# Moving one attention step, one output copy, two matmul slices and one transpose in a fused retention and hard-swish MLP kernel

## The chip, the core and the metric

The kernel runs on one NeuronCore of a Trainium2 chip. The metric is the device time of one execution in microseconds, and the number compared is the median of several runs. TensorE (PE) multiplies matrices and writes to PSUM banks; VectorE (DVE) and ScalarE (ACT) work elementwise and copy PSUM to SBUF; GpSimd (POOL) issues the loads, which change float32 to float16 on the way; SyncE (SP) issues the stores and the transposing DMAs. Each engine runs its own list of instructions in order, and semaphores make one wait for another.

## The reference

Two stages in a row. The first is attention with a decay in place of a softmax (retention), for 8 batches, 8 heads, 576 positions and head size 64. Its output is the input of a two-layer MLP over 4608 tokens, with model width 512 and hidden width 2048:

```python
scores = scale * np.matmul(q, k.transpose(0, 1, 3, 2))
gamma = 1.0 - 2.0 ** (-5.0 - np.arange(H, dtype=np.float32))
rel = pos[:, None] - pos[None, :]
Dmat = np.where(rel >= 0, gamma[:, None, None] ** rel[None, :, :], 0.0)
x = np.matmul(scores * Dmat, v)          # reordered to (tokens, heads * head_dim)
h = x @ w_in
g = h * np.clip(h + 3.0, 0.0, 6.0) / 6.0
out = g @ w_out
```

## The kernel before

**Pieces and blocks.** Each batch's first 512 positions are cut into four pieces of 128; the last 64 positions of two batches make up one "rest" piece. Pieces 0 to 3 are batch 0, pieces 4 to 7 batch 1, pieces 8 to 11 batch 2, piece 12 the first rest piece. A block is 512 tokens: block 0 is pieces 0 to 3, block 1 is pieces 4 to 7. The attention of a piece writes its columns of `xt16`, the transposed input of the MLP, and a block can run when its four pieces stand there.

**Attention of one piece.** `transpose_k` and `transpose_q` (a DMA transpose on SP's queue, the second behind a scaling of Q and V on VectorE) or `k_by_pe` and `q_by_pe` (on TensorE, with a copy on ScalarE) bring K and Q into the tile `qk`. `scores` multiplies them into the PSUM tile `sc`; VectorE masks it into `at`; `intra` multiplies `at` with the scaled V (`vs`) into the PSUM tile `o`, which has one bank; the state of the earlier pieces (`tbd`) times Q is added to `o`; ScalarE copies `o` to `xt16` (L340). `update_mm` and `update_state` make the next state: matmuls into `u`, VectorE for `ta` and `ts`, then two ScalarE copies into a `tbd` tile (L387, L388).

**MLP of one block.** GEMM1 makes 16 hidden slices of 128 (`fc` 0 to 15): four matmuls into a bank of the PSUM tag `ph` (four banks), then a ScalarE activation and a VectorE product into `gt16`. GEMM2 makes four row tiles (`mc`), each of 16 matmuls, cut into four units of four (`part`); the last unit of a row tile is followed by a ScalarE copy to `osb` and a store on SP's queue. `put` runs a list of units, after each one at most one deferred piece of work (`run_later(1)`), and then the steps that stand under that unit's number.

**The order around the change.** While GEMM2 of block 0 runs, `first_step(c)` for c = 3 to 8 carries pieces 4 to 7 through the attention. Such a step finishes piece c - 1 (`intra`, `update_mm`, `update_state`, then the state matmuls at L550 and the copy), makes the scores of piece c, and prepares Q and K of piece c + 1. State copies and masks are put on the list `later` and come into the order of the engines when `run_later` is called. `first_step(7)` stands behind unit 15, the last of GEMM2 of block 0. Behind it come fc 0 and fc 1 of block 1 over the first 384 columns (`g1_columns` with `done`; these are pieces 4 to 6), then `first_step(8)`, which finishes piece 7, and then the rest of the first four slices, where `last` is piece 7's 128 columns. Fc 4 to 15 follow in `gemm1(1, ...)`, each with 512 columns; fc 4 takes the bank of fc 0. The transposes for pieces 8 and later go through SP's queue in program order, between the stores.

## Time and profile before

| what | value |
|---|---|
| three runs | 310.9, 312.09, 312.16 us; median 312.09 us |
| profiled execution, its own time | 311.0 us |
| its span, first to last instruction | 309.2 us |
| mean granted TensorE clock | 0.992 |
| VectorE, ScalarE, GpSimd busy | 60%, 56%, 35% of the span |

A profile is one execution, recorded by the hardware. Its time is 1.8 us more than its span, and lies 1.1 us under the median of the three runs. A busy row of TensorE includes the time until the last result is out, so that rows that follow each other overlap by about 0.2 us. The granted clock is the share of its full speed that TensorE was allowed in a stretch.

### The profile page before, as it was taken

The page shows a single profiled execution, that of the slowest core. Times are in us where ns is not written, and L with a number is a line of the kernel's source. Part 1 is how long each engine was busy: PE and PEld are TensorE (multiplying, and loading weights), DVE is VectorE, ACT ScalarE, POOL GpSimd, SP SyncE. Part 2 cuts the span into 40 slices and gives each one's busy share as a digit, 9 for nine tenths or more (in the row PEclk, how much of TensorE's full clock was granted, in tenths as well). Part 3 has the DMA queues.
Part 4 walks back from the last instruction along what each step waited for, and adds up shares of the span by engine and source line. Part 5 has one row for each costly group of instructions (what it writes and reads, how often), then busy time and mean ns, then how long its engine had stood idle before and what let it go on. Part 6 is the DMA issues. An engine that isn't in the chain of part 4 may idle for free.

```text
span 309.2 us, 5776 instructions
## 1 busy us (share of the span) xinstructions
PE 299.3 (97%) x2239; PEld 150.4 (49%) x2239; DVE 185.6 (60%) x309; ACT 174.4 (56%) x301; POOL 107.9 (35%) x134
## 2 busy tenths in 40 slices
PE   6999997999999999999999999999999999999994
PEld 2644454544544554445544644455445544444443
DVE  4768336497747872885578747857688347207700
ACT  5568357484457564854574737644774567227611
POOL 8963577536522392045333750158000000000000
PEclk9999999799999999999999999999999999999998
DMA  9999999999999999639999997199930120010022
GB/s 69 148 194 204 190 165 204 174 163 83 154 182 119 98 153 156 128 22 158 145 151 104 130 173 146 18 146 146 139 85 34 70 68 2 34 68 36 1 68 68
DMA packets 153163, 35.51 MB, mean 115 GB/s; under 512 B 143792, under 2 KB 148656, under 8 KB 153136
## 3 DMA queue, kind: packets, MB, share of 16 engines
q0 software_dynamic: 117264, 18.36, 82.1%
q1 hardware_dynamic: 35472, 16.26, 26.5%
q10 hardware_dynamic: 400, 0.52, 0.5%
q8 instruction: 17, 0.28, 0.4%
q14 instruction: 10, 0.08, 0.1%
HBM read 36.70 MB, written 9.44 MB: 149 GB/s over the span
## 4 chain that ended last, share of the span: by engine, by line
PE 93%; ACT 3%; DMA 1%; DVE 1%; issue 0%; POOL 0%; POOLq 0%; DVEq 0%; ACTq 0%
PE ph L400 39%; PE pout L458 39%; PE o L334 3%; PE sc L301 2%; PE o L323 2%; DMA qv<-in_q_dram 1%; PE u L358 1%; PE pout L471 1%; PE ph L423 1%; PE trq L224 1%; PE sc L571 1%; ACT qk L230 1%; ACT xt L340 1%; PE trk L215 0%; DVE at L244 0%
## 5 line engine op out<-in xcount | busy, mean ns | idle before, releaser
L408 DVE SCALAR_TENSOR_TENSOR gt<-u,ph 128x512 f16<-128x512 f32 x144 | 98.1, 687 | 64.5 <-ACT u L407 63.8
L458 PE MATMUL pout<-wout,gt 128*128 128x512 f16 x560 | 125.8, 379 | 0.0
L400 PE MATMUL ph<-xt,win 128*128 128x512 f16 x560 | 122.4, 379 | 0.2 <-DVE gt L408 0.2
L407 ACT ACTIVATE u<-ph,cb 128x512 f32<-128x512 f32 x144 | 98.3, 687 | 26.0 <-PE ph L400 24.3
L400 PEld LDWEIGHTS <-win 128*128 128x128 f16 x560 | 54.6, 98 | 66.2 <-DMA win<-in_moe_w_in_dram 0.4
L458 PEld LDWEIGHTS <-gt 128*128 128x128 f16 x560 | 52.7, 98 | 61.1
L91 POOL DMA_DIRECT2D kn<-in_k_dram x40 | 34.6, 867 | 96.0 <-PE u L358 76.9
L462 ACT COPY osb<-pout 128x512 f32<-128x512 f32 x35 | 20.5, 586 | 48.9 <-PE pout L458 48.6
L305 DVE TENSOR_TENSOR at<-sc,mask_wide 128x1024 f16<-128x1024 f32 x19 | 23.2, 1222 | 27.2 <-PE sc L301 27.1
L91 POOL DMA_DIRECT2D qv<-in_q_dram x40 | 34.5, 866 | 4.4 <-DMA wout<-in_moe_w_out_dram 3.1
L91 POOL DMA_DIRECT2D qv<-in_v_dram x40 | 34.6, 872 | 2.8 <-DMA wout<-in_moe_w_out_dram 1.7
L387 ACT COPY tbd<-ts 64x256 f16<-64x256 f16 x28 | 11.3, 405 | 33.7 <-DVE ts L371 16.9
L340 ACT CAST xt<-o 128x512 f16<-128x512 f32 x35 | 19.4, 588 | 7.5 <-PE o L334 4.1
L291 DVE TENSOR_TENSOR vs<-qv,gqv 128x1024 f16<-128x1024 f16 x28 | 17.9, 685 | 3.2 <-DMA qv<-in_v_dram 3.2
L579 DVE TENSOR_TENSOR at<-sc,mask_wide 128x512 f16<-128x512 f32 x24 | 15.3, 681 | 0.0
L334 PE MATMUL o<-at,vs 128*64 128x128 f16 x280 | 12.4, 225 | 0.2
L374 DVE TENSOR_TENSOR ta<-u,ts 128x256 f32<-128x256 f32 x21 | 8.7, 415 | 5.0 <-PE u L358 5.0
L388 ACT COPY tbd<-ts 64x256 f16<-64x256 f16 x28 | 11.2, 401 | 0.4
L334 PEld LDWEIGHTS <-vs 128*64 128x64 f16 x280 | 8.9, 111 | 3.8 <-DVE vs L202 1.3
L375 DVE TENSOR_TENSOR ts<-ta,gc 128x256 f16<-128x256 f32 x21 | 8.9, 425 | 1.7
L301 PE MATMUL sc<-qk 64*128 64x128 f16 x184 | 9.3, 222 | 0.6 <-ACT qk L230 0.5
L323 PEld LDWEIGHTS <-tbd 128*128 128x128 f16 x112 | 7.0, 98 | 4.0
(69 smaller groups left out, 119.3 us busy)
## 6 DMA issues: line engine op xcount, KB each, us to landing
out_dram<-osb SPq DMA_DIRECT2D x32, 256.0 KB, 4.2
kn<-in_k_dram POOLq DMA_DIRECT2D x32, 128.0 KB, 4.5
qv<-in_q_dram POOLq DMA_DIRECT2D x32, 128.0 KB, 4.8
qv<-in_v_dram POOLq DMA_DIRECT2D x32, 128.0 KB, 5.4
wout<-in_moe_w_out_dram POOLq DMA_DIRECT2D x4, 512.0 KB, 15.1
win<-in_moe_w_in_dram POOLq DMA_DIRECT2D x3, 512.0 KB, 10.0
win<-in_moe_w_in_dram POOLq DMA_DIRECT2D x2, 256.0 KB, 5.9
kn<-in_k_dram POOLq DMA_DIRECT2D x8, 64.0 KB, 4.5
```

Of the source, the lines that this page charges most:

```text
L91: nc.gpsimd.dma_start(dst[p0:p0 + n], src[b, :, s0:s0 + n, :].rearrange("h s d -> s h d"))
L291: nc.vector.tensor_tensor(out=vs, in0=loaded[c]["qv"], in1=gqv, op=ALU.mult)
L301: nc.tensor.matmul(sc[:, h2, p, :], qk[r, 1, p, :], qk[r, 0, p, :], start=True, stop=True)
L305: later.append(lambda: nc.vector.tensor_tensor(out=at.rearrange("t a b s -> t (a b) s"), in0=sc.rearrange("t a b s -> t (a b) s"), in1=mas ...
L334: nc.tensor.matmul(o[r, p, :], vs[:, 2 * p + h2, :], at[:, h2, p, :], start=(st[c]["first"] and p == 0), stop=(p == NPAIR - 1 and not more ...
L340: nc.scalar.copy(xt16[:, :, g0:g0 + P], o)
L400: nc.tensor.matmul(ph, win16[:, dmc, P * fc:P * fc + P], xt16[:, dmc, t0:t0 + MBLK], start=(dmc == 0), stop=(dmc == NCC - 1))
L407: nc.scalar.activation(u, ph, ACTF.Relu, bias=cb[:, 0:1], scale=1.0 / 6.0)
L408: nc.vector.scalar_tensor_tensor(out=gts[kb][:, fc, :], in0=u, scalar=1.0, in1=ph, op0=ALU.min, op1=ALU.mult)
L458: nc.tensor.matmul(pout, gt[:, fc, P * mc:P * mc + P], wout16[:, fc, :], start=(fc == 0), stop=(fc == NFC - 1))
L462: nc.scalar.copy(osb, pout)
L579: nc.vector.tensor_tensor(out=at[:, h2], in0=banks[h2], in1=mask[:, None, :].to_broadcast([P, NPAIR, P]), op=ALU.mult)
```

## The change

Four edits, all in the stretch between unit 14 of GEMM2 of block 0 and fc 4 of block 1.

- `first_step(7)` moves from behind unit 15 to behind unit 14. `transpose_k(8)` stays under unit 14, now written behind the step. On TensorE the four matmuls of unit 15 so follow the step in place of preceding it, and unit 15's copy to `osb` and its store follow the step's copies.
- In `first_step`, `run_later` for the state copies is no longer called ahead of the scores where there is no next piece to prepare (c = 7), and `scores` itself no longer calls it; it is called once, behind the copy of `o`. For c = 7, ScalarE's order becomes: copy of piece 6's output, then the two state copies of piece 6, then unit 15's output copy, then the copy of piece 7's output. For c = 4 to 6 the mask is called for later in the program, and the order on each engine stays as it was.
- The remaining parts of block 1's first four slices were ordered fc 2 `done`, fc 0 `last`, fc 3 `done`, fc 1 `last`, fc 2 `last`, fc 3 `last`. Now fc 1 `last` comes ahead of fc 3 `done`.
- `transpose_k(9)` moves from behind fc 4 of block 1 to behind unit 15. On SP's queue the order was K of 8, store of unit 15, Q of 8, K of 9, Q of 9; it becomes K of 8, store of unit 15, K of 9, Q of 8, Q of 9.

The orders on VectorE and GpSimd do not change.

```diff
-    def scores(c):
-        run_later(9)
+    def scores(c, late=9):
+        run_later(late)
...
         if new:
             q_by_pe(c + 1)
-        if old and c < 8:
+        if old and new:
             run_later(9)
         if EARLY <= c < 8:
-            scores(c)
-            run_later(9)
+            scores(c, 0)
         if old and before is not None:
             for p in range(NPAIR):
                 nc.tensor.matmul(o[:, p, :], tbd[before][:, p, :], st[c - 1]["qk"][:, 0, p, :],
...
         if old:
             copy()
+        if c < 8:
+            run_later(9)
         if EARLY <= c < 8:
             scale_v(c)
...
-         11: [(first_step, 5)], 13: [(first_step, 6)], 14: [(transpose_k, 8)], 15: [(first_step, 7)]})
+         11: [(first_step, 5)], 13: [(first_step, 6)], 14: [(first_step, 7), (transpose_k, 8)],
+         15: [(transpose_k, 9)]})
...
-    for fc, cols in ((2, done), (0, last), (3, done), (1, last), (2, last), (3, last)):
+    for fc, cols in ((2, done), (0, last), (1, last), (3, done), (2, last), (3, last)):
         g1_columns(1, fc, banks[fc], cols)
...
-    gemm1(1, {0: [(transpose_k, 9), (transpose_q, 9)], 1: [(transpose_k, 10)],
+    gemm1(1, {0: [(transpose_q, 9)], 1: [(transpose_k, 10)],
               4: [(transpose_q, 10)], 5: [(transpose_k, 11)], 8: [(transpose_q, 11)]})
```

## The prediction

> **What bounds the kernel now.** I read the page first, then TensorE's waits, the chain that ended last, and the windows and the timeline of the one stretch where TensorE stands still.

> ```profile
> span 309.2 us, 5776 instructions
> ...
> PE 299.3 (97%) x2239; PEld 150.4 (49%) x2239; DVE 185.6 (60%) x309; ACT 174.4 (56%) x301; POOL 107.9 (35%) x134
> ```

> TensorE is busy in 97% of the span, so a change of order can only win back its waits and its clock. TensorE's waits from 41 us to 62 us, the stretch that the change touches, are two:

> ```profile
> PE ph L423 <- ACT xt L340: 1.8, 1, 1.8
> PE ph L400 <- DVE gt L408: 0.2, 1, 0.2
> ```

> Windows of the same stretch, with one earlier (columns: stretch, length, busy TensorE with its instructions, granted clock, DMA share, GB/s):

> ```profile
> 10.50:13.91 3.41, 2.95 (x56) 1.00 2.36 151
> 48.04:51.46 3.42, 3.33 (x51) 1.00 1.84 242
> 51.46:54.87 3.41, 1.57 (x18) 1.00 2.13 157
> 54.87:58.28 3.41, 3.41 (x29) 0.50 2.06 191
> ```

> The wait of 1.8 us lies in the third; in the fourth the clock is at half, though TensorE is busy throughout. So the one wait costs twice: itself, and about 3.41 x 0.5 = 1.7 us of lost speed behind it. The chain (start, length, engine, tile, line) shows who sets the time:

> ```profile
> 42.54 1.73 PE pout L458 x8
> 44.27 0.34 PE o L334 x8
> 44.61 0.12 PE u L358 x8
> ...
> 50.37 0.50 ACT xt L340
> 50.87 0.04 issue
> 50.91 0.41 PE o L334 x8
> ...
> 52.89 0.40 ACT tbd L388
> 53.31 0.60 ACT xt L340
> 53.91 0.04 issue
> 53.95 1.85 PE ph L423 x8
> ...
> 57.12 1.52 PE ph L423 x8
> 58.69 0.04 issue
> 58.73 0.70 ACT u L407
> 59.45 0.70 DVE gt L408
> 60.15 0.04 issue
> 60.19 10.53 PE ph L400 x48
> ```

> The attention step for pieces 6 and 7 starts at 50.91, when the copy of piece 5's output has cleared its bank. Its own output copy stands on ScalarE behind two state copies (0.40 the second), ends at 53.91, and block 1's first slices wait for it. At 60.19 fc 4 of block 1 starts, and from there to the end of GEMM1 of block 1 TensorE is one unbroken row. I measure the change by when that fc 4 starts.

> **The change, part by part.** Durations at full clock: eight 512-column matmuls take 1.73 (first chain row), so 0.216 each, 0.865 for a unit of four; scaled by columns, 0.162 for 384 columns and 0.054 for 128. Only the first is a row; 384 columns do not occur here at full clock, so between 0.162 and the 0.216 of 512 columns, and I take the scaled value, because four 128-column ones at 0.054 (0.22) agree with half of the row of eight at 0.34 to 0.05 us.

> From TensorE's and VectorE's timelines:

> ```profile
> 48.93 1.89 PE L458 MATMUL pout<-wout,gt 128*128 128x512 f16 x8
> ...
> 51.71 0.40 PE L550 MATMUL o<-qk,tbd 128*128 128x128 f16 x4
> ```

> ```profile
> 52.36 1.22 DVE L305 TENSOR_TENSOR at<-sc,mask_wide 128x1024 f16<-128x1024 f32 x1
> 53.49 0.41 DVE L202 TENSOR_TENSOR vs<-qv,gqv 128x512 f16<-128x512 f16 x1
> ```

> *The step one unit sooner.* The eight matmuls at 48.93 are units 14 and 15. Now only unit 14 precedes the step: TensorE is free at 48.93 + 0.865 = 49.80. The step still starts at 50.91, because the ScalarE chain ahead of it does not contain unit 15. So this part brings a wait of 1.11 us where there was one of 50.91 - 50.66 = 0.25 us. The step's matmuls stream until 51.71 + 0.22 = 51.93; then unit 15 runs until 52.80.

> *The output's copy first.* The last result stands at 51.71 + 0.40 = 52.11, so the copy runs from 52.15 to 52.74 (0.59, from 0.60 in its row, less the issue). Block 1's first slices can start at 52.78, just as unit 15 ends: 52.80 instead of 53.95. TensorE stood still from 51.93 to 53.95, 2.02 us; that is gone, but 0.865 of it is paid for by the longer early wait, so the net here is 1.15. Queued behind the copy are the two state copies (until 53.55), and unit 15's output copy, one ScalarE copy of about 0.59 (to 54.15). The state copies' reader is the step of piece 7's second half at about 54.6: 1.0 us of cover, and without it each microsecond would be paid in full. The output copy frees a bank that fc 3 of block 1 takes at about 56; 1.9 us of cover.

> *The first slices.* Eight 384-column matmuls: 52.80 + 1.30 = 54.10. Step 8 needs piece 7's mask (53.58) and its scaled V (53.90), VectorE rows that do not move: met by 0.2. Step 8 at full clock is 0.34 + 0.12 + 0.22 = 0.68, to 54.78; result 0.18 later; copy 55.00 to 55.59. Meanwhile fc 2 takes 0.65, to 55.43, and fc 0's last slice waits until 55.63, 0.2 us idle.

> *First two slices together.* Fc 0's end comes at 55.63 + 0.22 = 55.85 in either order; fc 1's comes 0.65 earlier than in the old order, fc 3's 0.22 later. Only fc 0 is on the path. ScalarE takes it at 56.05 (0.2 after the last matmul has streamed: the 0.18 from 51.93 to 52.11, and the issue), VectorE at 56.77, and fc 4 starts at about 57.50. The other matmuls end at 57.15, so 0.35 is idle against the 0.2 of the second wait above. Value 0; its bounds are -0.2 (fc 1's bank earlier) and +0.2 (fc 3's later), neither with a reader that waits.

> *Sum.* 60.19 - 57.50 = 2.69 us. Of it 1.15 is the wait, and 1.54 the half clock that no longer follows. As a check, the same steps from 53.95 on, with half clock from 54.87 to 58.28, give 60.15 for the kernel before; with full clock throughout they give 58.6.

> *K of piece 9 ahead of Q of 8.* It moves past one transpose of SP's queue, and stands behind unit 15's store, whose copy ends at 54.15. K of 9 can go if its load is there (the load's issue, and SP's queue):

> ```profile
> L91 POOL DMA_DIRECT2D kn<-in_k_dram x1: 876/876/876, 44.7 to 44.7; - x1
> ...
> DMA to landing us min/median/max: 8.1/8.1/8.1
> ```

> ```profile
> 58.21 1.20 SPq L292 DMA_TRANSPOSE qk<-vs  x1
> ```

> The load lands at 52.8. So K of 9 is issued at about 54.5 and, at the 1.20 of a transpose, has left the queue by 55.75. Q of 8 was issued at 58.21, directly behind the scaling of Q and V of piece 8, which follows step 8; step 8 ended at 57.12 and now ends at 54.78, so that Q of 8 is due at about 56 and finds the queue free. Cost 0; if K's load were late, Q of 8 would wait as long, and its reader, the first scores behind GEMM1 of block 1, comes some 12 us later. No gain either, since no TensorE row waits for these transposes.

> [...]

> **The rivals.** *The early wait drops the clock too.* The 1.11 us now fall into one stretch; had they fallen into the second window above, its busy time would be 3.33 - 0.86 = 2.47 of 3.42, or 72%. The rows bracket the limit: 46% (1.57) was followed by half clock, 86% (2.95) was not. 72% lies nearer the safe end, and the window's phase can split the wait. If the clock drops at 51.46: the step ends at 52.40, its copy 53.21, unit 15 54.13, slices 55.80, step 8 56.48, copy 57.24, fc 0 57.5, fc 4 59.15. That is 1.04 us saved.

> *The gain is eaten later.* TensorE comes 2.69 us earlier to loads that do not. The latest is V of piece 11:

> ```profile
> L91 POOL DMA_DIRECT2D qv<-in_v_dram x1: 883/883/883, 53.4 to 53.4; - x1
> ...
> DMA to landing us min/median/max: 8.4/8.4/8.4
> ```

> It lands at 61.8. Its first reader, the scaling for piece 11, stands behind fc 12 of block 1, which was due at 60.19 + 9 x 0.865 = 68.0 and now comes at 65.3: 3.5 us remain. Loads later by that and 2.7 us more would leave no gain, 311.0.

> *Slower: the clock falls early and stays down.* Place: from 51.46 on. Price: about 1.7 us of lost work per further window of half clock. One window leaves the 1.04 above; by the same steps with doubled TensorE times, two put fc 4 at 60.8, 0.6 later than before; three at 61.6, four at 63.3. From the second on the kernel is slower, from the fourth by over 0.5%. Against it: the window 54.87:58.28 was at half clock and fully busy, and the 48 matmuls from 60.19 ran at 10.53 / 48 = 0.22 each, full clock.

> **How the numbers follow.** The profiled execution took 311.0, 1.8 beyond its span; the three runs shown are 310.9, 312.09 and 312.16, so their median is 1.1 above it. The sum gives 311.0 - 2.7 = 308.3 against the profiled execution and 309.4 against the median; runs of both kinds will come again, so I say 308.9, halfway. With the same 0.55 the rivals give 310.5 (one window), 311.6 (no change) and 312.2 to 314.7 (slower). Chances: forecast 0.62, early clock drop 0.28, eaten 0.05, slower mechanism 0.05. What this measurement can tell from no change is about 0.5%, 1.56 us: the forecast is beyond it, the first rival (1.0) within. So faster 0.64 (the forecast and a little of the rival), same 0.31, slower 0.05. The forecast's own range is 307.9 to 309.8 (the runs' spread of 1.2, and up to 0.5 for 384-column matmuls nearer 0.216); for 8 in 10 the upper end takes in most of the first rival: 307.8 to 310.9.

> **What would show it.** Right: no clock below 1.00 between 45 and 62 us; a TensorE wait of about 1 us before the step's first o matmul at 50.9, for the copy of piece 5; none before L423's first matmul; unit 15's four matmuls directly behind the step's L549; fc 4 at about 57.5. Wrong: a window at 0.50 behind that wait, then about 310.5; or a wait for transposed Q or K, or for a load, behind 60 us. If other executions of the kernel before had no half clock, the gain would shrink to about 1.1.

## The result and the profile after

| | kernel before | changed kernel |
|---|---|---|
| median | 311.47 us (7 runs, 310.39 to 312.76) | 309.03 us (7 runs, 308.81 to 309.92) |
| profiled execution, its span | 311.0, 309.2 us | 308.84, 307.0 us |

The ratio is 0.9927, with a 95% interval of 0.9901 to 0.9953, so the gain is clear of noise. TensorE's waits in the changed kernel, from 42 us to 63 us:

```profile
PE o L334 <- ACT xt L340: 1.0, 1, 1.0
PE ph L400 <- DVE gt L408: 0.2, 1, 0.2
PE trq L224 <- DMA qv<-in_q_dram: 0.2, 1, 0.2
```

The wait of 1.8 us behind the step is gone, and one of 1.0 us ahead of it has come. Windows of the changed kernel, 3.41 us each like the half clock of before, and in step with its own clock's records (columns: stretch, length, busy TensorE with its instructions, clock, DMA share, GB/s):

```profile
49.50:52.92 3.42, 2.46 (x35) 1.00 2.14 193
52.92:56.33 3.41, 3.39 (x38) 1.00 2.39 150
56.33:59.74 3.41, 3.17 (x27) 1.00 2.48 183
```

The first of them holds the whole new wait: TensorE is busy in 2.46 of 3.42 us, 72%, and the two windows behind it are at 1.00. The chain that ended last, in the same stretch:

```profile
50.74 0.50 ACT xt L340
51.24 0.04 issue
51.28 0.41 PE o L334 x8
51.69 0.12 PE u L358 x5
51.82 0.33 PE sc L301 x8
52.15 0.33 PE o L549 x4
52.48 0.86 PE pout L458 x4
53.34 1.30 PE ph L423 x8
54.64 0.34 PE o L334 x8
...
56.11 0.40 PE ph L423 x4
...
58.05 4.04 PE ph L400 x18
```

Between the step and block 1's slices no other engine stands in the chain any more: unit 15's four matmuls (52.48) lead straight to L423. From the step's first matmul to fc 4 of block 1 it is 58.05 - 51.28 = 6.77 us, where it was 60.19 - 50.91 = 9.28. That distance is the measure for the experiments, because it does not contain what differs between executions further up (the step itself started 0.37 later here; the wait for a load, the third of the waits above, is part of that). The rest, from fc 4 to the end, is 249.0 us in both. SyncE's queue has K of 9 ahead of Q of 8, neither of them late:

```profile
54.58 0.34 SPq L443 DMA_DIRECT2D out_dram<-osb  x1
55.02 1.29 SPq L286 DMA_TRANSPOSE qk<-kn  x1
56.74 1.25 SPq L292 DMA_TRANSPOSE qk<-vs  x1
```

### The profile page after: what moved, and what is told of

Same layout as the page of the kernel before. It is cut to its first block, busy times and chain, and to the rows that moved or that the text cites. A ratio compares the mean times of both kernels' runs of the same rounds, so it can differ in the third digit from the quotient of the medians.

```text
span 307.0 us, 5776 instructions
## 1 busy us (share of the span) xinstructions
PE 298.3 (97%) x2239; PEld 150.1 (49%) x2239; DVE 185.8 (61%) x309; ACT 174.7 (57%) x301; POOL 107.9 (35%) x134
## 4 chain that ended last, share of the span: by engine, by line
PE 83%; DMA 8%; POOL 5%; ACT 2%; DVE 1%; issue 0%; POOLq 0%; ACTq 0%
PE pout L458 37%; PE ph L400 35%; DMA wout<-in_moe_w_out_dram 4%; DMA qv<-in_q_dram 4%; PE o L334 3%; POOL qv L91 2%; PE sc L301 2%; PE o L323 2%; PE u L358 1%; POOL kn L91 1%; POOL win L95 1%; PE pout L471 1%; PE sc L572 1%; PE ph L423 1%; ACT qk L216 0%
## 5 line engine op out<-in xcount | busy, mean ns | idle before, releaser
L408 DVE SCALAR_TENSOR_TENSOR gt<-u,ph 128x512 f16<-128x512 f32 x144 | 98.1, 688 | 63.6 <-ACT u L407 62.9
L458 PE MATMUL pout<-wout,gt 128*128 128x512 f16 x560 | 126.0, 379 | 0.0
L400 PE MATMUL ph<-xt,win 128*128 128x512 f16 x560 | 122.3, 379 | 0.2 <-DVE gt L408 0.2
L407 ACT ACTIVATE u<-ph,cb 128x512 f32<-128x512 f32 x144 | 98.3, 688 | 25.4 <-PE ph L400 24.2
L400 PEld LDWEIGHTS <-win 128*128 128x128 f16 x560 | 54.7, 98 | 66.0 <-issue 0.4
L458 PEld LDWEIGHTS <-gt 128*128 128x128 f16 x560 | 52.7, 98 | 60.8
L91 POOL DMA_DIRECT2D kn<-in_k_dram x40 | 34.5, 865 | 91.8 <-PE u L358 72.6
L305 DVE TENSOR_TENSOR at<-sc,mask_wide 128x1024 f16<-128x1024 f32 x19 | 23.2, 1223 | 27.6 <-PE sc L301 27.4
L91 POOL DMA_DIRECT2D qv<-in_q_dram x40 | 34.2, 861 | 6.4 <-DMA wout<-in_moe_w_out_dram 3.3
L91 POOL DMA_DIRECT2D qv<-in_v_dram x40 | 34.6, 870 | 2.8 <-DMA wout<-in_moe_w_out_dram 1.7
L340 ACT CAST xt<-o 128x512 f16<-128x512 f32 x35 | 19.4, 589 | 6.4 <-PE o L334 4.0
L334 PE MATMUL o<-at,vs 128*64 128x128 f16 x280 | 12.4, 225 | 1.1 <-ACT xt L340 1.0
L388 ACT COPY tbd<-ts 64x256 f16<-64x256 f16 x28 | 11.3, 403 | 0.4
L334 PEld LDWEIGHTS <-vs 128*64 128x64 f16 x280 | 8.9, 111 | 4.4 <-DVE vs L202 2.1
```

The source lines that it names most:

```text
L91: nc.gpsimd.dma_start(dst[p0:p0 + n], src[b, :, s0:s0 + n, :].rearrange("h s d -> s h d"))
L305: later.append(lambda: nc.vector.tensor_tensor(out=at.rearrange("t a b s -> t (a b) s"), in0=sc.rearrange("t a b s -> t (a b) s"), in1=mas ...
L334: nc.tensor.matmul(o[r, p, :], vs[:, 2 * p + h2, :], at[:, h2, p, :], start=(st[c]["first"] and p == 0), stop=(p == NPAIR - 1 and not more ...
L340: nc.scalar.copy(xt16[:, :, g0:g0 + P], o)
L400: nc.tensor.matmul(ph, win16[:, dmc, P * fc:P * fc + P], xt16[:, dmc, t0:t0 + MBLK], start=(dmc == 0), stop=(dmc == NCC - 1))
L407: nc.scalar.activation(u, ph, ACTF.Relu, bias=cb[:, 0:1], scale=1.0 / 6.0)
```

## The experiments

Two sessions of four kernels, each with 12 executions, beside 35 of the kernel before (median 311.17 in the first session, e1 to e4, and 310.65 in the second, e5 to e8). The medians of the first two rows are those of the result above, so that a median is best compared within its session. The distances from the step to fc 4, each from two rows of that kernel's chain (e7 and e8, which move the step's start itself, are measured from an earlier step and follow below):

| kernel | step starts, fc 4 starts | distance | median |
|---|---|---|---|
| before | 50.91, 60.19 | 9.28 | 311.47 |
| changed | 51.28, 58.05 | 6.77 | 309.03 |
| e1: copy first alone | 51.33, 58.08 | 6.75 | 309.01 |
| e2: step one unit sooner alone | 51.65, 59.57 | 7.92 | 310.44 |
| e3: before, wait filled | 51.18, 59.10 | 7.92 | 310.09 |
| e4: step and copy, slices and K as before | 52.58, 59.36 | 6.78 | 309.17 |
| e5: changed, early wait filled | 52.60, 59.30 | 6.70 | 309.48 |
| e6: step two units sooner | 51.50, 60.83 | 9.33 | 311.28 |

**e1, the copy alone.** In the kernel before, the edit to `first_step` and `scores` alone:

```diff
-    def scores(c):
-        run_later(9)
+    def scores(c, late=9):
+        run_later(late)
...
-        if old and c < 8:
+        if old and new:
             run_later(9)
         if EARLY <= c < 8:
-            scores(c)
-            run_later(9)
+            scores(c, 0)
...
         if old:
             copy()
+        if c < 8:
+            run_later(9)
```

> The kernel before with one edit alone: the copy of piece 6's output ahead of its two state copies; the step stays behind unit 15. Theory (the sum of the prediction): fc 0 of block 1 waits for that copy alone, which ends 1.15 us sooner, so TensorE's wait behind the step shrinks from 1.84 to about 0.65 us by the profile, the early wait stays at about 0.2, the clock stays at 1.00, and the time is that of the whole change, 309.0, 2.5 below the kernel before (311.5). Rival (the gain comes from unit 15 covering the copy): without the cover the wait stays in the main, and the time is 310.5 or more.

Measured: 309.01 (ratio 0.9943, 0.9920 to 0.9967). TensorE's waits in the stretch, and the chain around the copy:

```profile
PE ph L423 <- ACT xt L340: 0.7, 1, 0.7
```

```profile
51.33 0.41 PE o L334 x8
...
52.56 0.59 ACT xt L340
...
53.20 1.46 PE ph L423 x8
...
58.08 4.05 PE ph L400 x18
```

The copy starts 1.23 us behind the step's start, where it took 53.31 - 50.91 = 2.40 before. Fc 0 starts 1.87 us behind the step's start, and fc 4 comes as soon as in the changed kernel. TensorE waits 0.7 here behind the step in place of 1.0 ahead of it. The whole of the gain is in this one edit, and the rival has fallen.

**e2, the step alone.**

```diff
-         11: [(first_step, 5)], 13: [(first_step, 6)], 14: [(transpose_k, 8)], 15: [(first_step, 7)]})
+         11: [(first_step, 5)], 13: [(first_step, 6)], 14: [(first_step, 7), (transpose_k, 8)]})
```

> The kernel before with one edit alone: the step of pieces 6 and 7 one unit sooner, state copies still ahead of the output's copy. Theory: fc 0 of block 1 starts no sooner than before, since the copy still ends at 53.9; the one wait of 1.84 us is split in two, about 1.0 before the step and 1.0 behind unit 15. The sum of the waits is as before; if the split keeps the clock at 1.00, the time is 309.9 (1.5 below 311.5), and if not, 311.5. Rival (moving the step is what brings the gain): 309.0.

Measured: 310.44 (ratio 0.9979, 0.9954 to 1.0004). Waits of the stretch, and windows:

```profile
PE ph L423 <- ACT xt L340: 1.0, 1, 1.0
PE o L334 <- ACT xt L340: 0.9, 1, 0.9
```

```profile
49.64:53.05 3.41, 2.46 (x38) 1.00 2.12 204
53.05:56.47 3.42, 2.44 (x28) 1.00 2.32 149
56.47:59.88 3.41, 3.15 (x40) 1.00 2.81 163
```

The waits add up to as much as in the kernel before, in two parts, and in this execution they fell into two windows, busy to 72% and 71%, with the clock up. The distance of 7.92 is that of a kernel that waits as before without losing clock. The rival's 309.0 was not reached. The median lies 0.5 above the 309.9 that was expected with the clock up. In the profiled execution (310.40 us, mean clock 1.000) the clock is not the reason: its step starts at 51.65, 0.47 later than the 51.18 of e3, which has the same distance and took 309.89. Other executions of the 12 have mean clocks down to 0.988; whether some of them ran a window at half clock here was not recorded.

**e3, the wait filled.** In the kernel before, ahead of block 1's first slices:

```diff
+    for _ in range(8):
+        nc.tensor.matmul(banks[1], zeros[:, 0:P], zeros, start=True, stop=True)
```

> The kernel before, with eight matmuls of zeros by zeros (512 columns, into the bank of fc 1, which the first real matmul overwrites) put between the step of pieces 6 and 7 and fc 0 of block 1. They fill TensorE's wait of 1.84 us and change nothing else. Theory (the half clock comes from the idle time): the clock stays at 1.00 after it, fc 0 starts at 53.95 as before, fc 4 about 1.5 us sooner, time 309.9 to 310.0. Rival (the half clock has another cause, such as the loads or the point of time): half clock as before, 311.5.

Measured: 310.09 (ratio 0.9991, 0.9961 to 1.0020). Windows and chain:

```profile
50.35:53.76 3.41, 3.32 (x40) 1.00 2.32 160
53.76:57.17 3.41, 3.27 (x35) 1.00 1.87 196
```

```profile
51.18 0.41 PE o L334 x8
...
53.59 0.59 ACT xt L340
54.23 1.46 PE ph L423 x8
...
59.10 2.97 PE ph L400 x13
```

The copy ends as late as before, fc 0 starts 3.05 behind the step as before (53.95 - 50.91 = 3.04), and yet fc 4 comes 9.28 - 7.92 = 1.36 us sooner, for nothing but a clock that stays up. So 1.36 is the price of the half clock between these two profiled executions. That the filling kept the clock up is not settled by this trace alone. Its windows begin elsewhere relative to the step; without the zeros the first of them would have been busy for about 1.95 us (an estimate: 3.32 less the 1.54 of the zeros in it, and 0.16 until the last real result is out), 57%, and a window of 57% in e4 was followed by full clock (last section). The executions speak for the filling: 10 of e3's 12 took 310.48 us or less, and 13 of the 35 of the kernel before in the same session. That the half clock goes with the idle time is shown by e6 below, where a wait of 1.8 us stands at another place and the half clock follows it there (52.64 to 56.06).

The ratio to the kernel before is not clear of 1, because not every execution of that kernel pays the price. Of its 70 executions in both sessions, 27 had a mean granted clock of 0.997 or more, and their median is 310.28; the other 43 have 311.46. This split is rough, since the mean does not say where the clock was lost: ten of the 43 took 310.3 or less, and three of the 27 took 311.2 or more. Two of the 12 of e3 took over 312, with mean clocks of 0.992 and 0.993, and no trace shows where.

**e4, the slices and K of piece 9 taken back.** The changed kernel with

```diff
-         11: [(first_step, 5)], 13: [(first_step, 6)], 14: [(first_step, 7), (transpose_k, 8)],
-         15: [(transpose_k, 9)]})
+         11: [(first_step, 5)], 13: [(first_step, 6)], 14: [(first_step, 7), (transpose_k, 8)]})
...
-    for fc, cols in ((2, done), (0, last), (1, last), (3, done), (2, last), (3, last)):
+    for fc, cols in ((2, done), (0, last), (3, done), (1, last), (2, last), (3, last)):
...
-    gemm1(1, {0: [(transpose_q, 9)], 1: [(transpose_k, 10)],
+    gemm1(1, {0: [(transpose_k, 9), (transpose_q, 9)], 1: [(transpose_k, 10)],
```

> The changed kernel with two of its edits taken back: block 1's slices in the old order (fc 3's first part ahead of fc 1's last) and K of piece 9 behind Q of piece 8 again. Theory: both are worth nothing, so 309.0 within 0.3, and fc 4 of block 1 starts as far behind the step as in the changed kernel (6.8 us). Rival (fc 1's bank comes free earlier and shortens the path): 309.3 or more, with a wait of a later slice on VectorE's product.

Measured: 309.17 (ratio 0.9935, 0.9911 to 0.9960), distance 59.36 - 52.58 = 6.78 against 6.77, and the same 0.2 us of waiting for fc 0's product. Both edits together are worth nothing that these runs can tell.

**e5, the early wait filled.** The changed kernel, with five such matmuls ahead of `first_step(7)`, into the bank of fc 0 (the four banks of block 1's first slices are named there already).

> The changed kernel, with five matmuls of zeros by zeros (512 columns, into the free bank of fc 0) ahead of the step of pieces 6 and 7, in the 1.0 us that TensorE waits there for piece 5's copy. Theory: that wait by itself starts nothing late and does not drop the clock, so the time is that of the changed kernel, 309.0 within 0.3, and fc 4 starts 6.8 us behind the step. Rival (the early wait costs clock in some of the executions): the filled kernel is faster in the median by 0.3 or more, and no mean clock under 0.99 is left.

Measured: 309.48 (ratio 0.9962, 0.9938 to 0.9986). The early wait is gone and the distance is 6.70; counted from the step before, 59.30 - 49.01 = 10.29 us against 58.05 - 47.82 = 10.23. So filling it wins nothing, and the rival has fallen. The median came out 0.45 above that of the changed kernel, more than the 0.3 expected. The two medians are of different sessions, and this stretch does not show why they differ. The profiled execution (310.1 us) starts the step 1.32 later than that of the changed kernel, and it lost clock elsewhere, in the first 15 us:

```profile
8.33:15.15 6.82, 5.90 (x57) 3.74 (x57) 4.39 (x6) 2.76 (x5) 6.82 (x10) 0.50 2.25 147
```

(In this view the busy times of all five engines stand ahead of the clock.) A mean clock below 1 therefore does not by itself say that a window was lost at the step.

**e6, the step two units sooner.**

```diff
-         11: [(first_step, 5)], 13: [(first_step, 6)], 14: [(first_step, 7), (transpose_k, 8)],
+         11: [(first_step, 5)], 13: [(first_step, 6), (first_step, 7)], 14: [(transpose_k, 8)],
```

> The changed kernel with the step of pieces 6 and 7 yet one unit sooner, directly behind the step of pieces 5 and 6. Theory: the step still starts when piece 5's copy ends, so TensorE's wait there grows to about 1.9 us, and two units follow the step where the output's copy needs only 0.85 us of cover: fc 0 and fc 4 start 0.87 later, fc 4 7.6 us behind the step, 309.9 where the clock stays up; a wait as long as that of the kernel before also drops the clock in part of the executions, so a median of 310.0 to 311.2. Rival (a wait ahead of the step is harmless to the clock, whatever its length): 309.9 and no window at half clock.

Measured: 311.28 (ratio 1.0013, 0.9991 to 1.0036). Waits, windows and chain:

```profile
PE o L334 <- ACT xt L340: 1.8, 1, 1.8
```

```profile
45.82:49.23 3.41, 3.31 (x51) 1.00 2.00 228
49.23:52.64 3.41, 1.60 (x37) 1.00 2.06 207
52.64:56.06 3.42, 3.42 (x11) 0.50 2.46 142
56.06:59.47 3.41, 3.39 (x41) 1.00 2.98 147
```

```profile
51.50 0.41 PE o L334 x8
...
52.70 3.34 PE pout L458 x8
56.04 1.37 PE ph L423 x8
```

The wait ahead of the step has grown to 1.8 us, its window is busy to 47%, and the next one runs at half clock: eight matmuls take 3.34 us where they take 1.73. The distance is 9.33 - 6.77 = 2.56 longer than in the changed kernel: the expectation had 0.87 for the second unit, and the rest, 1.7, is the half clock. Together that gives back everything that the copy's new place had won. The median lies just above the 310.0 to 311.2 expected. So a wait of 1.8 us was followed by half clock ahead of the step (here, its window busy to 47%) as behind it (the kernel before, 46%), and the wait of 1.0 us ahead of the step, its window busy to 72%, was not (the changed kernel).

**e7 and e8, the same order in the steps before.** The sum says that after the change the step waits 1.1 us for piece 5's copy, which stands behind state copies in its own step. e7 is the changed kernel with this order in all the steps, and with V scaled first:

```diff
+        if old and c < 8:
+            scale_v(c)
         if old:
             before = state_of.get(b)
...
-        if old and new:
-            run_later(9)
...
-        if new:
-            k_by_pe(c + 1, "ph" if old else "tu")
         if old:
             copy()
+        if new:
+            k_by_pe(c + 1, "ph" if old else "tu")
         if c < 8:
             run_later(9)
-        if EARLY <= c < 8:
+        if c == EARLY:
             scale_v(c)
```

> The changed kernel with the same order in the steps before it: in the steps 5 and 6 too ScalarE's copy of the output comes first, then K's copy, then the two state copies, and VectorE scales V of the next piece ahead of the state's arithmetic. Theory: the step of pieces 6 and 7 no longer waits for piece 5's copy (about 0.8 us) but for its mask alone, and the step before it starts 0.25 sooner; about 1.0 us is won, 308.0. Rival (the chain of state, mask and scores on VectorE sets the step's start anyway): 308.8, with the wait at the step renamed to VectorE's mask.

Measured: 308.24 (ratio 0.9934, 0.9908 to 0.9960), the lowest median of the study, though three of its 12 executions took 310.16 to 310.40. The ratio, to the kernel before of its own session, is no lower than the changed kernel's 0.9927; that e7 is the faster of the two rests on the traces. No wait at the step is left in TensorE's list, and the chain reaches the step through VectorE:

```profile
48.59 0.44 DVE ta L374
49.02 0.02 issue
49.05 0.42 DVE ts L375
49.47 1.14 DVE at L305
50.61 0.04 issue
50.66 0.41 PE o L334 x8
```

Its fc 4 starts at 57.43. Counted from the step of pieces 4 and 5 (44.99), that is 12.44 us, against 58.05 - 44.63 = 13.42 in the changed kernel: 0.98 won, as the theory had it. What ends last now is the mask, as the rival said; but in the changed kernel the copy had stood 0.8 us behind it. There the scaling of V ended at 50.75, 0.5 ahead of the copy and behind the mask, so that by these rows its earlier place in e7 is needed for the whole of the gain; the two edits were not run apart.

e8 is e7 with the step behind unit 15 again.

> The kernel of e7 with the step of pieces 6 and 7 behind unit 15 again. Theory: now the step could start before unit 15 ends, so its place matters: fc 0 starts about 0.5 later than in e7, and TensorE waits about 0.65 for the output's copy; 308.5. Rival (as in e1, the place is worth nothing): the time of e7.

Measured: 308.91 (ratio 0.9944, 0.9919 to 0.9968); fc 4 58.17 - 45.12 = 13.05 us behind the step of pieces 4 and 5, 0.61 more than in e7, with TensorE waiting 0.7 for the copy:

```profile
PE ph L423 <- ACT xt L340: 0.7, 1, 0.7
```

The median is 0.4 above the 308.5 expected, and 0.67 above that of e7. Here the place of the step is worth what it was not worth in e1.

## Why the prediction was right

The time came out 0.13 us from the forecast, and part of that is luck. The sum's own figure for the profiled execution was 308.3, and that execution took 308.84: the step started 0.37 later, from causes further up, and fc 4 came 0.18 later behind it. The 308.9 was put halfway between that and a median over three runs, which over seven came out 0.6 lower. The parts of the sum fared as follows.

**The early wait.** Put at 1.11 us; from unit 14's start at 49.30 (49.30 + 0.865 = 50.17) to 51.28 it was 1.11, and its own row says 1.0. It came from the same copy as said, and did not bring the step forward.

**The output's copy first.** Fc 0 was to start 52.80 - 50.91 = 1.89 behind the step, and the chain row of e1 has it at 1.87, in place of 3.04. Gain 1.15 by the sum, 1.17 between e3 and e1 (7.92 - 6.75), both of which run at full clock there. The sum had 52.78 for the copy and 52.80 for unit 15 side by side, and so contained that the step's move pays for itself and no more; the prediction did not say that the move could be left out, which is what e1 showed.

**The slices, and K of 9.** Put at 0; e4 measured 6.78 against 6.77.

**The clock.** Put at 1.54, the term that was most off: 1.36 between the profiled executions (e3), and only in part of the executions. The prediction took the profiled execution of the kernel before as the usual one, and named the other case in its last line, with a gain of about 1.1. By the 70 executions, the change is worth 310.28 - 309.03 = 1.25 where the mean clock was 0.997 or more, close to the copy's 1.17, and 311.46 - 309.03 = 2.4 in the others, close to the two together (2.5). These compare sessions, and the others contain executions that lost clock elsewhere, so they are a sign and not a measurement. The 2.4 between the medians should then depend on how many executions of the kernel before drop the clock at the step: its median was 310.65 in the session in which 17 of 35 had a mean clock of 0.997 or more, and 311.17 in that with 10 of 35. How many of them dropped it at the step is not known.

**Fc 4.** Predicted 6.59 behind the step (57.50 - 50.91), measured 6.77. Up to fc 0 the sum holds, by TensorE's timeline of the changed kernel:

```profile
52.32 1.03 PE L458 MATMUL pout<-wout,gt 128*128 128x512 f16 x4
53.18 1.46 PE L423 MATMUL ph<-xt,win 128*128 128x384 f16 x8
54.57 0.41 PE L334 MATMUL o<-at,vs 128*64 128x128 f16 x8
```

Unit 15 starts 1.04 behind the step (the sum had 1.02) and fc 0 1.90 behind it (1.89). The chain's 52.48 and 53.34 are later because a row of the chain begins when the result of the row before is out. Half of the 0.18 is a gap of 0.09 between the end of the first slices (53.18 + 1.30 = 54.48) and step 8 at 54.57, where the sum let one follow the other at once. Another 0.06 lies between fc 0's last matmuls and ScalarE's activation: 56.59 - 56.11 = 0.48, where the sum had 56.05 - 55.63 = 0.42. The clock's term is too big for the same reason: it was what the sum left over, 2.69 - 1.15.

**The rivals.** The early wait did not drop the clock: windows busy to 72% (after; 72% and 71% in e2) were followed by full clock, those busy to 46% and 47% (before, e6) by half. So in this stretch the prediction's two rows, 46% and 86%, are joined by 47% on the one side and 71% on the other; the last section has two more windows between them. Nothing was eaten later: 249.0 us from fc 4 to the end in both. The half clock lasted one window both times that it followed such a wait (before, e6), and did not stay down. At the start of e5 it lasted two, 6.82 us, with TensorE busy for 5.90 of them, so a half clock of more than one window, as the slower rival had it, was seen, if not at this place.

## What to carry to other kernels

When TensorE waits for a copy, look first at what stands ahead of that copy in its engine's list: two state copies that nobody needed for another microsecond cost 1.2 us here, and putting them behind it was the whole gain. Covering a wait with work from ahead of it only moves the wait, unless the engine could have started sooner; the same move was worth nothing beyond e1, which leaves it out, and 0.6 us once the wait ahead of it was gone (e8 to e7). Price a TensorE wait together with the clock of the window behind it: split in two (e2) or filled (e3), it cost its own length here, in one piece of 1.8 us inside one window it cost another 1.4 in the profiled execution (9.28 - 7.92).

## What the runs showed of the hardware

```profile
4.86:8.27 3.41, 1.87 (x26) 1.00 2.01 128
8.27:11.68 3.41, 3.07 (x37) 0.50 2.27 145
17.11:20.52 3.41, 1.96 (x20) 1.00 1.20 185
20.52:23.94 3.42, 3.42 (x18) 1.00 1.24 206
```

A window busy to 55% was followed by half clock (e6), and one busy to 57% was not (e4). They hold other matmuls than the windows at the step, so the shares are comparable only as the profile counts them, and two single windows do not make a limit.

One wait of 1.8 us in one window was followed by half clock (the kernel before, e6); two waits of 0.9 and 1.0 us in two windows were not (e2).
